# The ninth chunk's attention product as 64x64 array quarters, with even and odd heads in two PSUM banks

## The chip, the cores and the metric

The kernel runs on one core of one Trainium2 chip. The time is device microseconds of that core, as the median of several executions. Before the change it is 264.96 us, the median of 3 runs (264.48 to 265.18). One execution was also recorded by the hardware profiler; its lines are quoted below. In them PE is TensorE's matmul row, PEld its weight loads, DVE is VectorE, ACT is ScalarE, POOL is GpSimd and SP is SyncE, whose queue issues DMAs.

## What is computed

There are 8 batches, 8 heads, 576 positions and a head dimension of 64. Attention here is linear: q is normalised over the head dimension, k over the positions, and the product of k and v is a 64x64 matrix per head. After it comes a layer norm with a two-layer MLP and a residual.

```python
# q, k, v: (8, 8, 576, 64) float32; moe_w_ch1: (512, 2048); moe_w_ch2: (2048, 512)
q_s = softmax(q, axis=-1)
k_s = softmax(k, axis=2)
kv = np.einsum('bhsd,bhse->bhde', k_s, v)
x = np.einsum('bhsd,bhde->bhse', q_s, kv)            # the ninth chunk's part of this is what changes
x = x.transpose(0, 2, 1, 3).reshape(8, 576, 512)
xn = (x - mu) / np.sqrt(var + 1e-06) * g_ln
out = x + np.maximum(xn @ w_ch1, 0.0) @ w_ch2
```

## The kernel before

**Chunks.** The 8 x 576 positions are worked in nine chunks of 512, each as 4 token tiles (t = 0 to 3) of 128 positions. Chunks 0 to 7 are the first 512 positions of each batch. The ninth chunk, `C9` (number 8), gathers the 64 positions that are left of each of the eight batches: its tile t holds batch 2t in partitions 0 to 63 and batch 2t+1 in partitions 64 to 127.

**The order.** It is written out by hand. `run(main, side)` walks through the MLP steps of one chunk (`mlp_steps`, weight 0.5 for each 128x128x256 matmul) and puts in, at the places that the side list names, the attention of the next chunk and the loads of the one after. Each engine executes its instructions in the order in which they were issued. C9's attention is the side list `attn_rest` (L870) while chunk 7's MLP is the main list. It puts `po_mm` of t = 0 and 1 at place 14 and of t = 2 and 3 at place 58, `x_fast` of the four tiles at 22, 54, 66 and 75, `square_sum` at 46, 62, 69 and 77, the DMA transposes `xn_T` at 61 and 78, and `sum_x` at 102.

**The attention product.** `po_mm(c, t, i)` (L380) multiplies the transposed exponentials `eqT` of one tile and one pair of heads i (partitions 0 to 63 hold the even head's 64 dimensions, 64 to 127 the odd head's) by `kv_sb[:, batch, i, :]`, a 128x128 matrix with the two heads' 64x64 blocks on the diagonal and zeros elsewhere. In chunks 0 to 7 that is one matmul with 128 rows, 128 columns of weights and 128 moving columns. In C9 the two halves of a tile belong to two batches, so there are two matmuls (L394): 128 rows, 64 columns of weights (one batch's 64 positions), 128 moving columns. A tile t of C9 fills one PSUM buffer `po` of [128, 512] float32, one bank. The pool `att_ps` (L69) has two such banks; `po` of t = 2 takes the bank of t = 0, and t = 3 that of t = 1.

**What follows it.** `x_fast(c, t)` (L424) is one DVE instruction that multiplies the bank by the reciprocal softmax sums `rq`, writes `x` in bf16 and its row sum into `mv[:, t, 0:1]`; the row sum comes as a second record, DVE_READ_ACCUMULATOR. `xn_out` (L416) then subtracts the mean. `square_sum` (L404, ACT) gives the variance, with that row sum as its bias. `xn_T` (L274) transposes `xn` by DMA from SP's queue, tiles 0 and 1 in one and 2 and 3 in the other. `sum_x` (L244) makes the four sums `tq` of C9's transposed `xn` on DVE.

**What stands beside it.** Both layers of the MLP use seven products in place of eight (`prod1` L698, L711; `prod` L552, L566) with sums of their operands. For the second layer, `sum_h` (L539, L550) makes the sums `hs` on DVE, `copy_u` (L589, L591) copies bank `ba` to SBUF on ACT, `add_u` (L593, L594) adds such a copy on DVE (`seed_e` begins bank `be` with it), and `y_quarter` (L572, L577) makes the output quarters from the banks. The pool `mm_ps` (L70) has six banks for these. The first layer of C9 begins right behind chunk 7's second layer: its second `bb` bank is the one in which chunk 7's `ba` was.

`kv_pairs` (L343, L357) is the other place with matmuls of 64 weight columns: the product of k and v, 128 rows, 64 columns of weights, 65 moving columns, the two halves of the array's columns in turn.

Of the kernel before, what the change touches and what calls it, by code (L numbers as in the profile page):

```python
# [12 lines left out]
FP32 = mybir.dt.float32  # L13
BF16 = mybir.dt.bfloat16
AF = mybir.ActivationFunctionType
ALU = mybir.AluOpType
# [4 lines left out]
def kernel(  # L21
# [16 lines left out]
    nc = tc.nc  # L38

    B, H, S, D = q.shape  # L40
    DM = H * D
    DH = 4 * DM
    P = 128
# [5 lines left out]
    NP = H // 2  # L49
# [3 lines left out]
    C9 = B  # L53
# [15 lines left out]
    att_ps = ctx.enter_context(tc.tile_pool(name="att_ps", bufs=2, space=PS))  # L69
# [19 lines left out]
    kv_sb = const.tile([P, B, NP, P], BF16)  # L89
# [85 lines left out]
    eks, eqs, eqTs, xs, xnTs, rstds, tqs = {}, {}, {}, {}, {}, {}, {}  # L175
# [165 lines left out]
    halves = (slice(0, 64), slice(64, P))  # L341
# [36 lines left out]
    pobox = {}  # L378

    def po_mm(c, t, i):  # L380


        if i == 0:
            pool, tag = (mm_ps, "m") if c == 0 and t >= 2 else (att_ps, "a")
            pobox["p"] = pobox[c, t] = pool.tile([P, DM], FP32, tag=tag, name="po")
        if c < B:
            nc.tensor.matmul(  # L387
                pobox["p"][:, i * P : i * P + P], eqTs[c][:, t, i, :], kv_sb[:, c, i, :],
                start=True, stop=True,
            )  # L390
        else:
            for half in range(2):
                ps = slice(64 * half, 64 * half + 64)
                nc.tensor.matmul(  # L394
                    pobox["p"][ps, i * P : i * P + P], eqTs[c][:, t, i, ps],
                    kv_sb[:, 2 * t + half, i, :], start=True, stop=True,
                )

    def stats(c, t, src):
        _, st, _, mv = xs[c]  # L400
# [15 lines left out]
    def xn_out(c, t):  # L416

        x, _, xn, mv = xs[c]
        nc.vector.tensor_scalar(
            out=xn[:, t], in0=x[:, t], scalar1=float(DM), scalar2=mv[:, t, 0:1],  # L420
            op0=ALU.mult, op1=ALU.subtract,
        )

    def x_fast(c, t):  # L424

        x, st, _, mv = xs[c]
        nc.vector.scalar_tensor_tensor(  # L427
            x[:, t].rearrange("p (h d) -> p h d", h=H),
            in0=pobox[c, t].rearrange("p (h d) -> p h d", h=H), scalar=1.0,
            in1=eqs[c][2][:, t].to_broadcast([P, H, D]), op0=ALU.mult, op1=ALU.mult,  # L430
            accum_out=mv[:, t, 0:1] if c else st[:, t, 0:1],
        )
        if c:
            xn_out(c, t)
# [394 lines left out]
    def attn_fast(c):  # L829

        s = [(4 + 4 * t, lambda t=t: reduce_q(3, t, 2)) for t in (0, 2)] if c == 3 else []
        kv, new, ps, squares, ts, rstd = (
            (24, 40, ((48, 53), (57, 59), (65, 67), (73, 75)), (66, 74, 87, 91), (61, 78), 95)
            if c == 3 else
            (3, 10, ((13, 24), (48, 53), (57, 59), (65, 67)), (60, 66, 74, 87), (55, 70), 92)
        )
        s += [(22 if c == 3 else 2, lambda: recip_q(c)), (kv, lambda: kv_pairs(c)), (new, lambda: start_x(c))]
        for t, (p0, p1) in enumerate(ps):
            s += spread([lambda t=t, i=i: po_mm(c, t, i) for i in range(NP)], p0, p1)
            s += [(p1, lambda t=t: x_fast(c, t)), (squares[t], lambda t=t: square_sum(c, t))]  # L840
        s += [(ts[0], lambda: xn_T(c, 0, 2)), (ts[1], lambda: xn_T(c, 2, 2)), (rstd, lambda: rstd_op(c))]
        s += [((84, 100 if c == C9 - 1 else 88, 92, 101)[i], lambda i=i: sum_x(c, i)) for i in range(4)]
        return s

    def second_side():

        s = [(p, lambda i=i: quarter_w2(i, 1)) for i, p in enumerate((7.8, 7.9, 33.9, 66))]
        s += [(8.0, lambda: xn_pT(1, 3, nc.vector))]
        s += [(3, lambda: exp_q(2, 0, 4)), (7, lambda: exp_q(2, 2, 4)), (7.2, lambda: eq_T(2))]
        s += [(40, lambda: square_sum(1, 2)), (63, lambda: square_sum(1, 3)), (67, lambda: rstd_op(1))]  # L850
        s += [(10, lambda: load_batch(3, (2,), eqTs[2][0:1, T - 1, NP - 1, 0:4])), (31, lambda: load_batch(3, (0,)))]
        s += [(23 + j, lambda j=j: cast_v(2, j)) for j in range(2)]
        s += [(at, lambda i=i: sum_x(1, i)) for i, at in enumerate((9.1, 9.2, 31.5, 36))]
        s += [(10.1, lambda: load_v(3))]
        s += [(101 + j, lambda j=j: cast_v(3, j)) for j in range(2)]
        s += [(15 + 3 * t, lambda t=t: reduce_q(2, t, 2)) for t in (0, 2)]
        s += [(36, lambda: recip_q(2))]
        s += [(18, lambda: exp_k(2, 0, 4)), (22, lambda: exp_k(2, 2, 4)), (26, lambda: prep_kvrem(2))]
        s += [(35, lambda: kv_pairs(2))]
        s += [(40, lambda: start_x(2))]  # L860
        for t, (p0, p1) in enumerate(((42, 45), (47, 52.6), (55, 60.5), (65, 69))):
            s += spread([lambda t=t, i=i: po_mm(2, t, i) for i in range(NP)], p0, p1)
            s += [(p1, lambda t=t: x_fast(2, t)), ((69, 78, 84, 90)[t], lambda t=t: square_sum(2, t))]
        s += [(57, lambda: xn_T(2, 0, 2)), (73, lambda: xn_T(2, 2, 2)), (96, lambda: rstd_op(2))]
        s += [(74, lambda: exp_q(3, 0, 4)), (78, lambda: exp_q(3, 2, 4)), (84, lambda: eq_T(3))]
        s += [(93, lambda: exp_k(3, 0, 4)), (104, lambda: exp_k(3, 2, 4)), (109, lambda: prep_kvrem(3))]
        s += spread([lambda i=i: sum_x(2, i) for i in range(4)], 95, 108)
        return s

    def attn_rest():  # L870

        s = [(2, lambda: recip_q(C9)), (4, lambda: start_x(C9))]
        for t, (p0, p1, p2) in enumerate(((14, 22, 46), (14, 54, 62), (58, 66, 69), (58, 75, 77))):
            s += [(p0, lambda t=t: [po_mm(C9, t, i) for i in range(NP)])]
            s += [(p1, lambda t=t: x_fast(C9, t)), (p2, lambda t=t: square_sum(C9, t))]
        s += [(61, lambda: xn_T(C9, 0, 2)), (78, lambda: xn_T(C9, 2, 2)), (88, lambda: rstd_op(C9))]
        return s + spread([lambda i=i: sum_x(C9, i) for i in range(4)], 102, 104)
# [274 lines left out]
```

## Time and profile before

| what | value |
|---|---|
| median of 3 runs | 264.96 us (264.48 to 265.18) |
| the profiled execution's own time | 264.57 us |
| its span, first to last instruction | 262.8 us |
| mean granted TensorE clock | 0.998 |
| C9's `po` matmuls (L394) | 32, in two bursts of 16, begun at 211.1 and 221.4 us |
| `x_fast` on a bank (L427) | 34 instructions 128x512, 683 ns each, and 34 READ_ACCUMULATOR, 82 ns each |
| from 210 to 225 us | PE busy 15.00 of 15.00, DVE 12.18, ACT 11.65, POOL 0.18 us |
| from 225 to 235 us | PE busy 10.00 of 10.00, DVE 8.71, ACT 2.95 us |

A busy record begins where its instruction starts and lasts until its end; matmuls overlap in the array, so the distance from one start to the next is what a matmul costs, and not its record of some 220 or 270 ns. The same holds for DVE: a 128x512 instruction has a record of 0.68 us, and the next one can start 0.61 us after it.

### The profile page before, as it was taken

What the parts mean: (1) busy time and instruction counts of PE and PEld (TensorE: products, weight loads), DVE (VectorE), ACT (ScalarE), POOL (GpSimd) and SP (SyncE); (2) the same over time, 40 slices, a digit from 0 to 9 for tenths busy, and PEclk for the clock granted to TensorE, in tenths of its full rate; (3) what the DMA queues carried; (4) which work ended last, traced back from release to release, by engine and by line L of the source; (5) the groups of instructions that cost most, each with busy time, mean ns of one, the idle gap of its engine ahead of it and who ended that gap; (6) DMA issues with size and microseconds to landing.
All of it is one profiled execution on the core that took longest, in us unless ns stands there. A gap on an engine that the chain in (4) does not pass through costs nothing.

```text
span 262.8 us, 6694 instructions
## 1 busy us (share of the span) xinstructions
PE 255.6 (97%) x2624; PEld 220.0 (84%) x2627; DVE 224.0 (85%) x492; ACT 174.3 (66%) x340; POOL 94.8 (36%) x148
## 2 busy tenths in 40 slices
PE   8999989999999999999999999999999999999993
PEld 6789745789888898999899889998899888888882
DVE  6879597999999999899889988998898869977872
ACT  4557780888977885789478947894788378447400
POOL 3962228233079104930980097009000800030000
PEclk9999999999999999999999999999999999999999
DMA  6999999979958995999299929994906320321014
GB/s 193 254 205 206 356 218 283 282 185 298 170 125 265 281 140 67 284 274 129 67 301 247 167 62 278 247 169 94 266 5 127 115 81 10 73 102 60 2 41 120
DMA packets 82536, 45.00 MB, mean 171 GB/s; under 512 B 58116, under 2 KB 79112, under 8 KB 82504
## 3 DMA queue, kind: packets, MB, share of 16 engines
q0 software_dynamic: 32464, 21.76, 44.2%
q1 hardware_dynamic: 49440, 22.29, 39.0%
q10 hardware_dynamic: 600, 0.53, 0.6%
q8 instruction: 20, 0.33, 0.5%
q14 instruction: 12, 0.10, 0.1%
HBM read 36.70 MB, written 9.44 MB: 176 GB/s over the span
## 4 chain that ended last, share of the span: by engine, by line
PE 82%; DMA 9%; POOL 3%; DVE 3%; ACT 1%; issue 0%; DVEq 0%
PE ba L566 21%; PE bx L711 20%; PE bb L711 10%; DMA qt<-in_q_dram 9%; PE be L566 5%; PE bc L566 5%; PE bb L566 5%; PE bc L711 5%; PE pc L519 3%; PE po L387 2%; PE pkv L357 2%; PE ph L483 1%; DVE x L427 1%; POOL w_raw L99 1%; DVE ot L500 1%; POOL v L965 1%
## 5 line engine op out<-in xcount | busy, mean ns | idle before, releaser
L566 PEld LDWEIGHTS <-hs 128*128 128x128 bf16 x512 | 49.8, 98 | 5.7
L711 PEld LDWEIGHTS <-w_q 128*128 128x128 bf16 x480 | 45.6, 98 | 5.1
L259 POOL TENSOR_TENSOR tq<-xnT 128x256 bf16<-128x256 bf16 x26 | 17.2, 677 | 77.0 <-DMA xnT<-xn 63.0
L566 PEld LDWEIGHTS <-hT 128*128 128x128 bf16 x384 | 37.1, 98 | 4.3
L711 PEld LDWEIGHTS <-w1g 128*128 128x128 bf16 x360 | 34.1, 98 | 4.1
L711 PE MATMUL bx<-tq,w_q 128*128 128x256 bf16 x240 | 31.7, 273 | 0.0
L566 PE MATMUL ba<-w_q,hs 128*128 128x256 bf16 x256 | 30.8, 273 | 0.0
L735 ACT COPY bc<-bx 128x512 f32<-128x512 f32 x30 | 16.7, 591 | 20.8 <-PE bx L711 20.5
L742 DVE TENSOR_TENSOR bb<-bx,s 128x512 f32<-128x512 f32 x30 | 19.5, 695 | 8.4 <-ACT s L739 5.7
L583 POOL DMA_DIRECT2D out_dram<-ot x28 | 15.4, 558 | 24.2 <-DVE ot L577 24.1
L427 DVE SCALAR_TENSOR_TENSOR x<-po,rq 128x512 bf16<-128x512 f32 x34 | 23.2, 683 | 0.9 <-PE po L387 0.7
L407 ACT ACTIVATE scrap<-x,mv 128x512 bf16<-128x512 bf16 x32 | 23.0, 720 | 1.4 <-DVE x L427 1.2
L753 ACT ACTIVATE hT<-bb 128x512 bf16<-128x512 f32 x30 | 16.3, 595 | 9.9 <-PE bb L711 9.1
L745 DVE TENSOR_TENSOR hT<-bx,s 128x512 bf16<-128x512 f32 x30 | 19.3, 684 | 3.8 <-PE bx L711 3.8
L387 PE MATMUL po<-kv_sb,eqT 128*128 128x128 bf16 x128 | 22.1, 219 | 0.0
L550 DVE TENSOR_TENSOR hs<-hT 128x1024 bf16<-128x1024 bf16 x32 | 21.6, 685 | 0.5 <-ACT hT L753 0.5
L753 ACT ACTIVATE hT<-bc 128x512 bf16<-128x512 f32 x30 | 16.4, 595 | 8.4 <-PE bc L711 8.4
L218 DVE TENSOR_REDUCE zq<-eq 128x16 f32<-128x1024 bf16 (+1 forms) x20 | 20.7, 1051 | 0.0
L591 ACT COPY s<-ba 128x512 f32<-128x512 f32 x15 | 8.7, 582 | 13.3 <-PE ba L566 8.6
L753 ACT ACTIVATE hT<-bx 128x512 bf16<-128x512 f32 x30 | 16.4, 604 | 0.7 <-PE bx L711 0.7
L566 PE MATMUL ba<-w_sb,hT 128*128 128x256 bf16 x128 | 16.7, 273 | 0.0
L739 ACT COPY s<-bb 128x512 f32<-128x512 f32 x30 | 16.5, 619 | 0.0
(152 smaller groups left out, 550.3 us busy)
## 6 DMA issues: line engine op xcount, KB each, us to landing
out_dram<-ot POOLq DMA_DIRECT2D x30, 256.0 KB, 5.0
qt<-in_q_dram SPq DMA_DIRECT2D x5, 1024.0 KB, 6.7
kt<-in_k_dram SPq DMA_DIRECT2D x5, 1024.0 KB, 12.2
qt<-in_q_dram POOLq DMA_DIRECT2D x2, 1024.0 KB, 12.4
kt<-in_k_dram POOLq DMA_DIRECT2D x2, 1024.0 KB, 14.1
vm<-in_v_dram POOLq DMA_DIRECT2D x16, 128.0 KB, 12.6
w_raw<-in_moe_w_ch_dram POOLq DMA_DIRECT2D x3, 512.0 KB, 10.4
w_sb<-in_moe_w_ch_dram POOLq DMA_DIRECT2D x3, 512.0 KB, 16.2
```

The costliest lines, as they stand in the source:

```text
L218: nc.vector.reduce_sum(eqs[c][1][:, ts], eqs[c][0][:, ts], axis=AX.X)
L259: eng.tensor_tensor(out=dst[:, t], in0=x[:, t], in1=y[:, t], op=ALU.subtract)
L387: nc.tensor.matmul(pobox["p"][:, i * P : i * P + P], eqTs[c][:, t, i, :], kv_sb[:, c, i, :], start=True, stop=True,)
L407: nc.scalar.activation(scrap, x[:, t], AF.Square, bias=mv[:, t, 0:1], scale=-float(DM), accum_out=mv[:, t, 1:2],)
L427: nc.vector.scalar_tensor_tensor(x[:, t].rearrange("p (h d) -> p h d", h=H), in0=pobox[c, t].rearrange("p (h d) -> p h d", h=H), scalar=1. ...
L550: nc.vector.tensor_tensor(out=dst, in0=x, in1=y, op=op)
L566: nc.tensor.matmul(hbox[bank][:, t], lhsT, rhs, start=first and (own or t == 0) and k == 0, stop=k == KH - 1, skip_group_check=True)
L711: nc.tensor.matmul(dst[:, q], lhsT, rhs, start=first and q == 0 and ko == 0, stop=ko == 1, skip_group_check=True)
L735: nc.scalar.copy(at[g, "c"], at[g, "x"])
L742: nc.vector.tensor_tensor(out=at[g, "b"], in0=at[g, "x"], in1=at[g, "s"], op=ALU.add)
L745: nc.vector.tensor_tensor(out=h_out(g, 1, 1), in0=at[g, "x"], in1=at[g, "s"], op=ALU.add)
L753: nc.scalar.activation(h_out(g, odd, half), at[g, name], AF.Relu)
```

## The change

For C9 alone, `po_mm` does one head of one batch at a time: 64 rows (one head's dimensions, `hs`), 64 columns of weights (one batch's positions, `tok`), 64 moving columns (that head's block of `kv_sb`). The row half is given by the head's place in the pair, the column half by the batch's half of the tile, so that the four matmuls of a pair lie in four different quarters of the array. There are 64 of them for 32 before. The even heads' results go to one bank and the odd heads' to another, so a pair of tiles (t = 0 and 1, or 2 and 3) fills two banks together, both of `att_ps`: t = 2 and 3 need both banks that t = 0 and 1 filled.

`x_fast` for C9 then reads two banks: two instructions of 128x256 (as 4 heads of 64, with `x` and `rq` strided), each with a row sum of its own in `st`, and one 128x1 addition of the two. For the other chunks nothing is different.

```diff
     def po_mm(c, t, i):
+        if c == C9:
+            if i == 0 and t % 2 == 0:
+                pobox["q"] = [
+                    att_ps.tile([P, 2, NP, D], FP32, tag="a", name="po") for _ in range(2)
+                ]
+            pobox[c, t] = pobox["q"]
+            for m, tok in enumerate(halves):
+                for half, hs in enumerate(halves):
+                    nc.tensor.matmul(
+                        pobox["q"][half][tok, t % 2, i, :], eqTs[c][hs, t, i, tok],
+                        kv_sb[hs, 2 * t + m, i, hs], start=(t % 2 == 0 and i == 0), stop=True,
+                        skip_group_check=True,
+                    )
+            return
         if i == 0:
             pool, tag = (mm_ps, "m") if c == 0 and t >= 2 else (att_ps, "a")
             pobox["p"] = pobox[c, t] = pool.tile([P, DM], FP32, tag=tag, name="po")
-        if c < B:
-            nc.tensor.matmul(
-                pobox["p"][:, i * P : i * P + P], eqTs[c][:, t, i, :], kv_sb[:, c, i, :],
-                start=True, stop=True,
-            )
-        else:
-            for half in range(2):
-                ps = slice(64 * half, 64 * half + 64)
-                nc.tensor.matmul(
-                    pobox["p"][ps, i * P : i * P + P], eqTs[c][:, t, i, ps],
-                    kv_sb[:, 2 * t + half, i, :], start=True, stop=True,
-                )
+        nc.tensor.matmul(
+            pobox["p"][:, i * P : i * P + P], eqTs[c][:, t, i, :], kv_sb[:, c, i, :],
+            start=True, stop=True,
+        )
...
     def x_fast(c, t):
         x, st, _, mv = xs[c]
+        if c == C9:
+            for half in range(2):
+                nc.vector.scalar_tensor_tensor(
+                    x[:, t].rearrange("p (i two d) -> p i two d", two=2, d=D)[:, :, half],
+                    in0=pobox[c, t][half][:, t % 2], scalar=1.0,
+                    in1=eqs[c][2][:, t].rearrange("p (i two) -> p i two", two=2)[:, :, half]
+                    .to_broadcast([P, NP, D]),
+                    op0=ALU.mult, op1=ALU.mult, accum_out=st[:, t, half : half + 1],
+                )
+            nc.vector.tensor_add(mv[:, t, 0:1], st[:, t, 0:1], st[:, t, 1:2])
+            xn_out(c, t)
+            return
         nc.vector.scalar_tensor_tensor(
```

## The prediction

> **What bounds the kernel now.** I read the page's busy shares and slices first, then the chain of waits in order of time, then the timeline around the two bursts of C9's `po` matmuls.
>
> ```profile
> PE 255.6 (97%) x2624; PEld 220.0 (84%) x2627; DVE 224.0 (85%) x492; ACT 174.3 (66%) x340; POOL 94.8 (36%) x148
> PE   8999989999999999999999999999999999999993
> DVE  6879597999999999899889988998898869977872
> PEclk9999999999999999999999999999999999999999
> ```
>
> PE is full from the second slice to the last but one, at full granted clock. That row alone proves little, because matmul records overlap. The chain (start, length, what) shows that PE's own work sets the time:
>
> ```profile
> 211.22 0.57 PE po L394 x16
> ...
> 221.50 0.57 PE po L394 x16
> ...
> 226.97 1.75 PE bc L566 x16
> 228.72 1.75 PE ba L566 x16
> ```
>
> From 208 to 258 us it names nothing but PE, and a common matmul's slot is 1.75/16 = 0.109 us. So in this stage time saved or lost on PE reaches the end; DVE and ACT count only where PE comes to wait for them.
>
> **Part 1, the bursts on PE.** The timeline at the first burst, and the first and last lines of the last `kv_pairs`:
>
> ```profile
> 210.62 0.60 PE L711 MATMUL bc<-xnT,w1g 128*128 128x256 bf16 x4
> 211.15 0.64 PE L394 MATMUL po<-kv_sb,eqT 128*64 128x128 bf16 x16
> 211.72 0.61 PE L711 MATMUL bc<-xnT,w1g 128*128 128x256 bf16 x4
> ```
>
> ```profile
> 182.53 0.32 PE L357 MATMUL pkv<-vm,ek 128*64 128x65 bf16 x8
> ...
> 183.16 0.20 PE L357 MATMUL pkv<-vr,ekr 128*64 128x65 bf16 x2
> ```
>
> The last `bc` matmul ahead of the burst starts at 210.62 + 0.60 - 0.27 = 210.95, and its slot ends at 211.06. PE is back at common matmuls at 211.72. The burst therefore costs 0.66 us. Its 16 matmuls start over 0.64 - 0.22 = 0.42 us, 28 ns apart on average, about 0.45 us for all. The other 0.21 us is the way into this array shape and out of it, which I keep: the shape changes just as often.
>
> After the change a burst is 32 matmuls of 64 moving columns, in eight groups of four quarters. No row shows quarters. The nearest is `pkv`: 38 starts in 183.16 - 182.53 = 0.63 us, so 33 ns for a pair that fills both column halves with 65 moving columns, 16.6 ns each. If all four quarters run side by side, as the two column halves do, a group costs what such a pair does: 8 x 0.033 = 0.26, and with 0.21 a burst is 0.48 us, **0.18 us less**. Bounds: 0.21 us, if the matmuls cost nothing beyond the change of shape (0.45 less); 32 x 0.033 + 0.21 = 1.27 us, if each takes a pair's slot alone (0.61 more). Between them, 16.6 ns each as in `pkv`, if only two run at a time: 0.53 + 0.21 = 0.74, 0.08 more. I take 0.48, as operands, banks and quarters of four neighbours are all different.
>
> The Trainium skill (TensorE: Matmul & The Clock Gate, "Wait — 56ns, not 53.3ns?") speaks against this: starts are said never to come closer than about 25 ns, however few columns move. By that rule a burst would be 32 x 25 ns + 0.21 = 1.01 us and the two together 0.7 us longer. The `pkv` row, at 16.6 ns, is already below that floor, so it does not hold between parts of the array here; what it would give is weighed below as a mechanism of its own.
>
> **Part 2, `x_fast` on DVE.** The timelines of DVE at the second tile, and early on, where L312 has the same operation with 128x128:
>
> ```profile
> 220.71 0.68 DVE L427 SCALAR_TENSOR_TENSOR x<-po,rq 128x512 bf16<-128x512 f32 x1
> 221.32 0.08 DVE L427 DVE_READ_ACCUMULATOR x<-po,rq 128x1 f32 x1
> 221.44 0.35 DVE L419 TENSOR_SCALAR xn<-x,mv 128x512 bf16<-128x512 bf16 x1
> ```
>
> ```profile
> 11.59 0.35 DVE L312 SCALAR_TENSOR_TENSOR kv_sb<-pkv,rzk,diag 128x128 bf16<-128x128 f32 x1
> 11.86 0.09 DVE L312 DVE_READ_ACCUMULATOR kv_sb<-pkv,rzk,diag 128x1 f32 x1
> 11.98 0.25 DVE L316 TENSOR_SCALAR mbc<-ones_w,kvs 128x128 bf16<-128x128 bf16 x1
> ```
>
> From the start of `x_fast` to that of `xn_out`, 0.73 us. A 128x512 takes 0.61 until its accumulator is read, a 128x128 0.27; 128x256 by the straight line is 0.39 (L577's 128x256 follow each other by 0.40). The read costs the next instruction nothing where that does not need it (at 17.79 us it and L891 start together) and 0.12 where it does; between the halves I take 0.06. The 128x1 addition needs both sums (0.12) and holds `xn_out` by about 0.15 (L445, 128x1, is 0.143). Sum: 0.39 + 0.06 + 0.39 + 0.12 + 0.15 = 1.11, **0.38 us more** for each tile; bounds 0.30 and 0.50.
>
> **Part 3, the new wait.** Before, t = 2 took a bank that had been free since 215.2 us, and only t = 3, eight matmuls into the second burst, needed the bank of t = 1, read until 221.40. Now the second matmul of the burst needs both banks. The work between the bursts follows PE: DVE and ACT idle there waiting for `bx` and `bb` (1.1 and 0.6 us), which also swallows the 0.38 of tile 0. So `x_fast` of tile 1 starts 0.18 earlier, at 220.53. It frees the odd heads' bank after 0.39 + 0.06 + 0.39 + 0.08 = 0.92, at 221.45, and PE goes on some 0.04 later (L419 starts 0.04 after the read's end). PE would be there at 221.43 - 0.18 = 221.25. **Wait 0.24 us** (0.16 to 0.36). Queued behind it on PE are the rest of the burst and chunk 7's `ba` products.
>
> **Part 4, DVE's debt.** Tiles 1 to 3 put DVE back by 3 x 0.38 - 0.18 = 0.96 us at 226, since it has no idle time from 217.3 to 228.3. Who waits:
>
> ```profile
> 226.03 0.72 ACT L407 ACTIVATE scrap<-x,mv 128x512 bf16<-128x512 bf16 x1 [1.21 <-DVE x L427]
> 226.65 0.19 ACT L407 ACTIVATION_READ_ACCUMULATOR scrap<-x,mv 128x1 f32 x1
> 227.01 0.59 ACT L591 COPY s<-ba 128x512 f32<-128x512 f32 x1 [0.17 <-PE ba L566]
> ```
>
> The square moves to 226.99, the copy behind it to 227.81, and `ba` is free at 228.40; PE wants it at 228.72 - 0.12 = 228.60. Cover 0.20, gone if a tile costs 0.45 more rather than 0.38. The seed of `be` (L594, ends 228.33) moves to 229.29, for PE at 230.35: cover 1.06. The sums `hs` begun at 221.71 are 0.2 late with 1.1 to spare. The transpose of tiles 2 and 3 leaves SP's queue 0.96 later, at 227.3; transposes land after 3.0 at the least, as this one did, so at 230.3. `sum_x` behind it starts at 230.3 for 229.55, four of them take 0.8, and DVE is 0.05 late at 231.12, where it had idled for ACT. The read of `ba` by L577 (ended 234.97) then clears C9's second `bb` bank by about 0.1 us. A landing 0.3 later costs PE 0.2. I cost Part 4 at nothing; without these covers, up to 0.6.
>
> **Sum:** -0.18 - 0.18 + 0.24 = **-0.12 us**. On the profiled execution, span 262.8, time 264.57, that is 264.45; its time is 0.39 below the median, so on the median it is 264.8.
>
> **Rivals.**
> - *The wait does not bite*, because the first half and its read overlap further than the rows show: -0.36, 264.6. For it: DVE starts instructions before the last one's record ends. Against: the bank's second half cannot be freed before the second instruction ends. The cheapest burst of the bounds gives -0.66, again with the wait away: 264.3.
> - *The debt surfaces on PE*, at the copy of `ba` or at the late transpose: +0.1 to +0.5, 265.1 to 265.5. For it: covers of 0.20 and 0.1. Against: several must be gone by tenths.
> - *Two at a time only*: 2 x 0.08 + 0.24 = +0.40, 265.4. For it: no row shows row halves side by side.
> - *One at a time, which ends slower.* A matmul in a quarter holds the array's issue until its 64 columns have moved: 28 ns, the average of a start in `po`, to 33. Its place is both bursts, 2 x (32 x 0.028 + 0.21 - 0.66) + 0.24 = +1.13, up to +1.46: 266.1 to 266.4. It decides against the change from 10 ns a matmul on (2 x 32 x 0.010 + 0.42 + 0.24 = 1.3, what the bursts cost now) and passes +0.8 from 23 ns. Against it: 16.6 ns in `pkv`, with two halves. The skill's floor would be this rival at 265.9.
>
> **How the numbers follow.** About 0.3%, 0.8 us, is what a measurement of this kernel can tell from no change. Forecast (-0.35 to +0.1) 0.47; the wait does not bite 0.12; debt 0.10; two at a time 0.10; one at a time 0.14; another loss over 0.8 that no row shows 0.03; a gain over 0.8 0.04, since both bursts together cost only 1.32 us. So faster 0.04, same 0.79, slower 0.17. Predicted 264.8. The range leaves out most of the one-at-a-time case and the last two: from 264.1 (the cheapest burst, and 0.2 of run-to-run spread) to 266.0.
>
> **What would show it.** A burst that costs 0.48 us from slot to slot, starts of four quarters together, groups 33 ns apart. In the second burst one or two matmuls at once, then a gap of about 0.2 us whose releaser is DVE's `x`. `x_fast` to `xn_out` 1.1 us for four tiles. The square of tile 3 on ACT at about 227.0 and no gap in `ba` at 228.6 nor in `bb` at 235. The prediction is wrong if a quarter's starts are over 20 ns apart throughout, or if PE stands still in 223 to 236 us.

## The result, and the profile after

The changed kernel takes 266.31 us (median of 8 runs, 264.07 to 268.04), the kernel before 264.92 us beside it (8 runs, 264.29 to 265.18). The ratio is 1.0045, 95% interval 1.0024 to 1.0066: about 1.2 us slower, where a gain of 0.12 us was forecast. The ratios of this document leave out runs that are over 1.5% longer than the fastest of their kernel, here the one of 268.04 us and later those of 268.81 and 269.06 us of h2_after_late64. The spread is as telling as the median: without that run still 3.3 us from the shortest to the longest, where the kernel before has 0.9.

The profiled execution of the changed kernel took 265.5 us, its span is 263.7 us and its mean granted clock 0.997. First its page: busy time by engine, slices of the span, and the row of a DMA queue, `q8 instruction`, that I take for the one that fetches PE's program (packets, MB, share of 16 DMA engines).

```profile
PE 255.8 (97%) x2659; PEld 220.4 (84%) x2659; DVE 224.3 (85%) x504; ACT 174.5 (66%) x340; POOL 94.8 (36%) x148
...
PE   8899999999999999999999999999999999999992
...
DVE  6778597999999999799879988998898979977872
...
PEclk9999999999999999999999999999999999999998
...
q8 instruction: 21, 0.34, 0.5%
```

PE has 35 matmul records more (32 were added; a few are missing from either trace) and 0.2 us more of busy time, DVE 0.3 us: nothing here looks like 1.2 us. The last line was not read in the prediction. The same row of the page before the change:

```profile
q8 instruction: 20, 0.33, 0.5%
```

So PE's program arrives in packets of about 16 KB, and there is now one more. That the queue is PE's follows from the runs below: rows added on PE move its packets or add one (g2_before_plus64, e3_pad_end), DVE instructions added do not (e2_dve_alone). Hold on to that row.

The chain of waits after the change (start, length, what), for the stage that the prediction spoke of:

```profile
211.75 0.44 PE bc L729 x4
212.18 0.38 PE po L391 x32
212.56 0.54 PE bc L729 x4
...
222.27 0.48 PE po L391 x32
...
227.66 1.75 PE bc L584 x16
229.41 1.75 PE ba L584 x16
```

It still names PE alone. The `bc` piece of 227.66 stood at 226.97 before, so PE is 0.69 us late there. It was already late ahead of both bursts. The PE timelines at the first and at the second burst:

```profile
211.58 0.60 PE L729 MATMUL bc<-xnT,w1g 128*128 128x256 bf16 x4
212.11 0.45 PE L391 MATMUL po<-kv_sb,eqT 64*64 64x64 bf16 x32
212.49 0.61 PE L729 MATMUL bc<-xnT,w1g 128*128 128x256 bf16 x4
```

```profile
221.67 0.60 PE L584 MATMUL ba<-w_sb,hT 128*128 128x256 bf16 x4
222.20 0.55 PE L391 MATMUL po<-kv_sb,eqT 64*64 64x64 bf16 x32
222.68 1.05 PE L584 MATMUL ba<-w_sb,hT 128*128 128x256 bf16 x8
```

Read as in the prediction, the slot ahead of the first burst ends at 211.58 + 0.60 - 0.27 + 0.11 = 212.02, and common matmuls go on at 212.49: the burst costs 0.47 us for 0.66 before. The second costs 222.68 - (221.67 + 0.60 - 0.27 + 0.11) = 0.57. Together the bursts are 0.28 us cheaper, wait included. But the first begins 0.97 us later than before (212.02 against 211.06), and this arose before 54 us, in code that the change doesn't touch. The end of the span adds 0.25 us: from DVE's last instruction to the end of the span it is 4.1 us for 3.85. 262.8 + 0.97 - 0.28 + 0.25 = 263.7, the span. So this profile shows a gain where the change is and losses in two places where it is not.

DVE's timeline at the second tile, whose odd-head half frees the bank that the second burst waits for:

```profile
221.49 0.42 DVE L435 SCALAR_TENSOR_TENSOR x<-po,rq 128x256 bf16<-128x256 f32 x1
221.83 0.08 DVE L435 DVE_READ_ACCUMULATOR x<-po,rq 128x1 f32 x1
221.83 0.42 DVE L435 SCALAR_TENSOR_TENSOR x<-po,rq 128x256 bf16<-128x256 f32 x1
222.17 0.08 DVE L435 DVE_READ_ACCUMULATOR x<-po,rq 128x1 f32 x1
222.29 0.16 DVE L442 TENSOR_TENSOR mv<-st 128x1 f32<-128x1 f32 x1
222.49 0.35 DVE L425 TENSOR_SCALAR xn<-x,mv 128x512 bf16<-128x512 bf16 x1
```

The halves start 0.34 us apart, and `xn_out` follows 1.00 us after `x_fast` began, for 0.73 before.

### The profile page after: what moved, and what is told of

It reads as the page before. It is cut to its first block, busy times and chain, and to the rows that moved or that the text cites. A ratio compares the mean times of both kernels' runs of the same rounds, so it can differ in the third digit from the quotient of the medians.

```text
span 263.7 us, 6773 instructions
## 1 busy us (share of the span) xinstructions
PE 255.8 (97%) x2659; PEld 220.4 (84%) x2659; DVE 224.3 (85%) x504; ACT 174.5 (66%) x340; POOL 94.8 (36%) x148
## 4 chain that ended last, share of the span: by engine, by line
PE 79%; DMA 12%; DVE 4%; POOL 3%; issue 0%; ACT 0%; DVEq 0%; ACTq 0%
PE ba L584 21%; PE bx L729 20%; PE bb L729 10%; DMA qt<-in_q_dram 9%; PE be L584 5%; PE bc L584 5%; PE bb L584 5%; PE bc L729 5%; DMA ktr<-in_k_dram 3%; PE po L400 2%; PE pkv L357 2%; PE ph L501 1%; DVE x L445 1%; POOL w_raw L99 1%; DVE ot L518 1%; POOL v L983 1%
## 5 line engine op out<-in xcount | busy, mean ns | idle before, releaser
L445 DVE SCALAR_TENSOR_TENSOR x<-po,rq 128x512 bf16<-128x512 f32 x30 | 20.5, 684 | 0.9 <-PE po L400 0.7
```

The lines of the kernel that those rows point to most:

```text
L445: nc.vector.scalar_tensor_tensor(x[:, t].rearrange("p (h d) -> p h d", h=H), in0=pobox[c, t].rearrange("p (h d) -> p h d", h=H), scalar=1. ...
```

## The experiments

All ratios are against the kernel before, run on the same chip. One count is useful beside the medians: runs over 265.5 us. Of the kernel before, 14 of 124 runs were over it (all together, median 264.73); of the changed kernel 13 of the 20 that the result and the first experiment give (median 265.87).

### The first set: which part carries the loss

**e1_again**: the changed kernel once more, no edit, to see whether the loss at 54 us and that at the end come back.

> The changed kernel again. Its profile had saved about 0.18 us around the two bursts, and lost 0.9 us before 54 us, in code the change does not touch, where loads landed later. If that loss belongs to the changed program (layout), it comes back: median about 266.3, ratio about 1.004 to 1.005, and the profile again 0.5 to 1 us late at the first ph matmul (54.3 for 53.3). If the first 54 us merely vary from run to run in any kernel, the ratio is 0.998 to 1.001 and the spread is that of the kernel before.

Measured 265.69 us (264.24 to 267.04, 12 runs), ratio 1.0027 (1.0005 to 1.0049). Its profiled execution, 266.22 us, is only 0.13 late at the first burst and has an end of the usual length. It loses its time at a third place. The timeline of DVE, the last part in brackets being the idle time ahead:

```profile
228.79 0.87 DVE L595 SCALAR_TENSOR_TENSOR ot<-bc,rstd,x 128x256 f32<-128x256 f32 x2
231.95 0.49 DVE L259 TENSOR_TENSOR tq<-xnT 128x256 bf16<-128x256 bf16 x2 [2.29 <-issue]
...
235.74 0.86 DVE L595 SCALAR_TENSOR_TENSOR ot<-ba,rstd,x 128x256 f32<-128x256 f32 x2
```

and of PE behind it:

```profile
233.65 1.04 PE L729 MATMUL bx<-xnT,w1g 128*128 128x256 bf16 x8
235.87 0.60 PE L729 MATMUL bb<-tq,w_q 128*128 128x256 bf16 x4 [1.19 <-DVE ot L595]
236.66 0.60 PE L729 MATMUL bb<-tq,w_q 128*128 128x256 bf16 x4 [0.19 <-DVE ot L595]
```

DVE stands still for 2.29 us ahead of `sum_x`, which reads the late transpose; the reads of the banks (L595) come behind it, the last of them frees the bank in which C9's second `bb` goes, and PE waits for that. This is the path of Part 4. What is late is the transpose. The DMA view of 226 to 234 us for this execution (GB/s in slices of 0.2 us, the queues, median us from issue to landing):

```profile
GB/s 0 0 0 0 0 0 0 0 0 0 0 90 218 223 207 205 192 158 17 84 0 0 0 0 0 0 0 0 0 0 0 0 0 0 0 0 0 0 0 0
...
q8 instruction: 1, 0.02, 0.7%
issues: line engine op xcount, KB each, median us to landing
xnT<-xn SPq DMA_TRANSPOSE x1, 4.8
```

The same view of the kernel before:

```profile
GB/s 0 0 0 0 0 0 0 40 211 219 214 204 206 183 35 0 0 0 0 0 0 0 0 0 0 0 0 0 0 0 82 0 0 0 0 0 0 0 0 0
...
xnT<-xn SPq DMA_TRANSPOSE x1, 3.0
```

The lone 82 of the kernel before, in the slice that begins at 232.0, is the packet of PE's program (16 KB in 0.2 us is 82 GB/s; it is booked where it starts, at 232.09). The transpose had ended 2.7 us earlier. In e1_again the packet is the 84 at 229.8, right at the transpose's end. The trace gives each part of the transpose a landing: in the kernel before all sixteen come from 229.24 to 229.40 us, in e1_again fifteen from 230.14 to 230.28 and one at 231.87. The packet lasts from 229.85 to 230.78. The same view of 229.84 to 230.84 us, in slices of 25 ns, shows what the late part waits for:

```profile
DMA  9000000000000000000000000000000000000100
...
q8 instruction: 1, 0.02, 5.8%
q1 hardware_dynamic: 2, 0.00, 0.3%
```

The program's packet begins at 229.852, as the last 256-byte packet of the transpose ends (229.856). The two packets of the transpose (q1) that are left have 4 bytes each; they begin at 230.769 and 230.778, just as the program's packet ends (230.783), and the late landing follows. Theory from here on: the 64 more PE rows (32 matmuls and 32 weight loads) shift the places where PE's program is fetched, DVE's debt shifts the transpose, and they meet.

**e2_dve_alone**: the kernel before, with `x_fast` of C9 in two halves and the addition, but on one bank and with the old matmuls. It carries DVE's debt without the quarters and without the extra rows.

```diff
     def x_fast(c, t):
+        if c == C9:
+            for half in range(2):
+                nc.vector.scalar_tensor_tensor(
...
+                    in0=pobox[c, t].rearrange("p (i two d) -> p i two d", two=2, d=D)[:, :, half],
...
+            nc.vector.tensor_add(mv[:, t, 0:1], st[:, t, 0:1], st[:, t, 1:2])
```

> DVE part alone: the old 128x64 matmuls into one bank for each tile, x_fast in two halves and the addition. By my sum: t = 3's bank is free 0.38 later, the wait for it at most 0.2 us, the bursts unchanged: 265.0 to 265.3. If the program's layout sets the early loads, it may be off by up to 1.5 us in the first 54 us, with only 8 more DVE instructions. If the cost of the change lies in x_fast, it is as slow as the changed kernel, 266.3.

Measured 264.57 us (264.0 to 266.06, 12 runs), ratio 0.9992 (0.9971 to 1.0013). The transpose lands from 229.98 to 230.12, the packet comes at 232.07, PE doesn't wait. The debt alone costs nothing.

**e3_pad_end**: the kernel before, with 32 matmuls of no use behind the last product (64 more PE rows at the end of the program).

```diff
+        pad = att_ps.tile([P, 64], FP32, tag="a", name="pad")
+        for _ in range(32):
+            nc.tensor.matmul(pad[0:64], junk[:, 0:64], junk[:, 0:64], start=True, stop=True)
```

> The kernel before with 32 more small matmuls at the very end of PE's program, behind the last product, beside the last stores: nothing before 258 us differs but the length of PE's program (64 rows, as many as the change adds). Layout theory: median 265.8 to 266.8 and a wider spread, loss in the first 54 us. Otherwise 264.9, same as before within 0.1%.

Measured 265.86 us (264.43 to 268.05, 12 runs), ratio 1.005 (1.0029 to 1.0071), 10 of 12 runs over 265.5. The matmuls themselves end at 259.2 us, before the last stores have landed. The DMA view of 256 to 266 us:

```profile
q8 instruction: 1, 0.02, 0.6%
issues: line engine op xcount, KB each, median us to landing
...
out_dram<-yl SPq DMA_DIRECT2D x2, 64.0 KB, 3.9
out_dram<-yl ACTq DMA_DIRECT2D x2, 64.0 KB, 4.2
```

and of the kernel before, which has no program packet there:

```profile
out_dram<-yl SPq DMA_DIRECT2D x2, 64.0 KB, 2.3
out_dram<-yl ACTq DMA_DIRECT2D x2, 64.0 KB, 2.8
```

A 21st packet (259.95 to 260.94) runs beside the last stores, and one landing in sixteen of the last four stores comes 1.4 to 1.8 us late (of the first, 262.05 with the other fifteen by 260.22). This is a second place where the extra rows cost time, with no quarter and no DVE debt in the kernel.

**e4_null**: the kernel before with its lines moved by 18 and nothing else.

> The kernel before with only its line numbers moved by 18. Both theories: 264.9, ratio 0.999 to 1.001. If it is as slow or as spread as the changed kernel (264 to 268), then building and loading a program anew already moves the time by that much, and neither the change nor its length is the cause.

Measured 264.77 us (264.0 to 266.59, 12 runs), ratio 1.0006 (0.9988 to 1.0025): moved source lines cost nothing.

### The second set: moving the packets

A helper issues n matmuls of no use in the four quarters. Put at place 73.9 of chunk 0's MLP (about 33 us, where PE has time to spare), 32 of them move every later packet by 64 rows.

```diff
+        def pad_mm(n):
+            pad = [att_ps.tile([P, 64], FP32, tag="a", name="pad") for _ in range(2)]
+            for i in range(n):
+                hs, tok = halves[i % 2], halves[i // 2 % 2]
+                nc.tensor.matmul(
+                    pad[i % 2][tok], junk[hs, 0:64], junk[hs, 0:64], start=True, stop=True
+                )
...
+                (73.9, lambda: pad_mm(32)),
```

**g4_after_plus64**: the changed kernel with `pad_mm(32)`.

> The changed kernel with those 32 small matmuls more (64 PE rows). Fetch theory: pieces at about 226, 239 and 254, ahead of the late transpose (227 to 231) and of the last stores: 264.4 to 264.9, less than the changed kernel by 1 us or more, with more instructions. Otherwise as the changed kernel or later, 265.7 to 266.5.

Measured 264.14 us (263.62 to 264.61, 12 runs), ratio 0.9975 (0.9962 to 0.9988). Adding 32 useless matmuls makes the changed kernel 1.5 us faster than e1_again (on another chip) and 0.6 us faster than the kernel before. In its profile the packets come at 224.69, 239.16 and 253.50, clear of the late transpose (landed 229.67 to 229.82) and of the last stores. It is also 0.20 us early at the first burst.

**g2_before_plus64**: the kernel before with `pad_mm(32)`.

> The kernel before with 32 small matmuls more on PE at 33.5 us, where PE waits 0.66 us for ACT: the same PE length as the changed kernel, bursts and x_fast as before. Fetch theory: the piece of 232 us comes at about 229, on this kernel's last transpose (26.3 to 229.4 us), and a 21st at about 259, beside the last stores: 265.3 to 266.2 with a spread of 2 us or more. If the cost is in the bursts or in x_fast: 264.7 to 265.0.

Measured 264.73 us (263.98 to 267.64, 12 runs), ratio 1.0004 (0.9978 to 1.0031). The median of 265.3 to 266.2 that was expected did not come. The tail did: three runs over 265.5. The profiled one, 265.67 us, has the packet of 259.66 beside the last stores and a landing at 261.99 where the other fifteen end by 260.08. In the middle, the packet starts at 228.46 and the transpose lands from 228.77 to 228.91, with no part late: the two meet without DVE's debt as well. The extra rows alone, so placed, hit now and then only. Why e3_pad_end, with a packet at the same place of the end, moves the median and this run does not, was not seen.

**g3_before_plus128**: the same with `pad_mm(64)`.

> The kernel before with 64 small matmuls more at the same place (128 PE rows). Fetch theory: pieces 7 us earlier, the late ones at about 225, 239 and 253, clear of the last transpose and of the last stores: 264.7 to 265.2 with the spread of the kernel before, though its program is longer than that of the changed kernel. If length itself costs (memory layout, more program to load), it is slower than the one with 64 rows more: 266 to 267.

Measured 265.32 us (264.33 to 266.89, 12 runs), ratio 1.0018 (0.9998 to 1.0038), a little above what was expected. Its profiled execution has its packets clear (225.77, 240.54, 254.25), no late landing, and is 0.24 us late at the first burst. Yet 4 of the 12 runs are over 265.5; what makes them longer was not seen, and it speaks against the packets as the only reason for long runs.

**g1_after_less64**: the changed kernel with 64 PE rows fewer, by leaving out the products ko 4 to 11 of chunk 0's second layer.

```diff
-                for t in range(T) for ko in range(k0, k0 + kn)
+                for t in range(T) for ko in range(k0, k0 + kn) if not 4 <= ko < 12
```

> The changed kernel with 64 PE rows fewer (32 weight loads, 32 matmuls): of chunk 0's second layer the products of ko = 4 to 11 are left out, at a place (35 to 49 us) where the loads set the pace. Fetch theory (PE's program comes in 16 KB pieces, about every 256 PE rows; the 64 added rows move the piece of 232 us onto the late transposes of tiles 2 and 3 and bring a 21st piece beside the last stores): the pieces are back where the kernel before has them, no 21st piece, so 264.4 to 264.7, ratio 0.998 to 1.000, spread under 1.5 us. If the change's own instructions (bursts, x_fast, debt) cost the time, it stays at 265.7 to 266.3.

Measured 271.8 us (270.88 to 272.37, 6 runs), ratio 1.0257 (1.0233 to 1.0282). This says nothing of the packets. The busy table by stage (us, PE busy with count, granted clock, DMA share, GB/s) of this run:

```profile
34.00:50.00 16.00, 7.87 (x51) 0.79 1.19 249
50.00:100.00 50.00, 47.89 (x530) 0.93 0.83 187
```

With PE idle for half of 34 to 50 us, the granted clock falls to 0.79 there and is 0.93 up to 100 us; in the profile of the changed kernel both stages have 1.00. Less work went with about 6 us more. A count of rows has to be changed where PE stays busy.

### The third set: one meeting at a time, and other ways to move

**h1_tile3_early**: `x_fast` of tile 3 at place 67.5 for 75 and its transpose at 70 for 78, so that the transpose is early; the length of the program is left as it is.

```diff
-        for t, (p0, p1, p2) in enumerate(((14, 22, 46), (14, 54, 62), (58, 66, 69), (58, 75, 77))):
+        for t, (p0, p1, p2) in enumerate(((14, 22, 46), (14, 54, 62), (58, 66, 69), (58, 67.5, 77))):
...
-        s += [(61, lambda: xn_T(C9, 0, 2)), (78, lambda: xn_T(C9, 2, 2)), (88, lambda: rstd_op(C9))]
+        s += [(61, lambda: xn_T(C9, 0, 2)), (70, lambda: xn_T(C9, 2, 2)), (88, lambda: rstd_op(C9))]
```

> The changed kernel with x_fast of tile 3 ahead of two of chunk 7's sums hs (place 67.5 for 75) and its transpose at place 70: the late transpose leaves SP 1.2 us earlier, at about 225.9, and lands at about 229, before the piece of PE's program at 230. The 21st piece at the end stays. If the loss of the changed kernel is at the transpose, 264.3 to 264.7; if it is at the last stores, 265.3 to 266; if each has a part, between.

Measured 264.64 us (264.15 to 267.17, 11 runs), ratio 1.0008 (0.9986 to 1.003); 2 of 11 runs over 265.5. The edit did not part the two: in its profile the transpose lands from 228.63 to 228.77, 1.2 us earlier than in i3_look below, but the packet comes 1.1 us earlier too, at 228.37. What it gives is more time for a late landing. The last packet comes at 263.58, after the end of the span.

**h2_after_late64**: the changed kernel with `pad_mm(32)` at place 14 of C9's own MLP (about 237 us), so that the packet near the transpose stays and the one at the end moves (to 254.13).

```diff
-        run(mlp_steps(C9), [(33 + 3 * i, lambda i=i: sum_h(0, i)) for i in range(2)])
+        run(mlp_steps(C9), [(33 + 3 * i, lambda i=i: sum_h(0, i)) for i in range(2)]
+            + [(14, lambda: pad_mm(32))])
```

> The changed kernel with 32 small matmuls more on PE inside C9's first layer (about 237 us), where PE sets the time: they cost 0.47 us as a burst does. The piece at 230 us stays where it is, beside the transpose; the last one moves from 258 to about 254.5, ahead of the last stores. If the end alone is the loss, 264.4 + 0.5 = 264.9 with a small spread; if the transpose is the loss, 265.9 to 266.5.

Measured 265.08 us (264.29 to 269.06, 12 runs), ratio 1.0016 (0.9991 to 1.0042); 5 of 12 runs over 265.5, four of them over 266.5. Of the 10 that the ratio counts, it is 3. The useless matmuls cost 0.47 us from slot to slot, 0.0018 of the ratio; less that, it is about 0.9998, beside 1.0008 in h1. Both expectations that named one place are missed, 265.9 to 266.5 for the transpose and a small spread for the end. With counts this small, neither run singles out a place.

**h3_both**: g4 and h1 together.

> Tile 3 early and the 64 more PE rows at 33.5 us together: transpose and last stores are both clear of the pieces, and the debt is smaller. 264.0 to 264.2, the same as with the 64 rows alone (264.14): nothing was left to gain at the transpose there.

Measured 264.2 us (263.62 to 264.77, 12 runs), ratio 0.9981 (0.9969 to 0.9994). With the packets clear, moving tile 3 adds nothing to g4.

**h4_warm18**: the changed kernel with 32 PE rows fewer and no work left out: the 34 warm-up matmuls at the start become 18 longer ones.

```diff
-    junk = const.tile([P, 256], BF16)
+    junk = const.tile([P, 512], BF16)
...
-        warm(34)
+        warm(18, 484)
```

> The changed kernel with 32 PE rows fewer, without leaving out work: the first warm-up as 18 matmuls of 484 columns for 34 of 256 (8712 columns for 8704). PE's program ends before a 21st piece, and the piece of 230 comes at about 231, behind the landing of the transpose. 264.2 to 264.6, spread under 1.5 us. If length does not matter, 265.7 to 266.3 as the changed kernel.

Measured 264.13 us (263.53 to 265.19, 12 runs), ratio 0.9983 (0.997 to 0.9995). The packet comes at 229.69, behind the landings of 229.23 to 229.37, and none is recorded at the end. It is 0.66 us early at the first burst. Of the 36 runs of g4, h3 and h4 none was over 265.5.

**i1_before_warm18**: the same warm-up in the kernel before.

> The kernel before with the warm-up as 18 matmuls of 484 columns, 32 PE rows fewer. If the gain of the changed kernel with that warm-up (264.13) comes from the quarters (0.1 to 0.2 us in the bursts, and nothing lost), this one is at 264.3 to 264.8. If the warm-up alone brings it, it is at 264.0 to 264.2.

Measured 264.57 us (264.01 to 266.19, 12 runs), ratio 1.0003 (0.9982 to 1.0024). The warm-up by itself brings no gain that this can tell. h4 is 0.44 us shorter, on another chip; the bursts explain 0.28 us of it, the rest is not shown.

**i2_look, i3_look, i4_look**: three single executions of the changed kernel, each with its profile.

> The changed kernel once more, for where a single execution loses time. Fetch theory: one over 265.3 us shows one of 16 landings of the late transpose over 1 us after the others, with a gap on PE at 234.5 to 237 behind it, or one landing of the last stores over 1 us after the others; one under 264.8 shows neither.

> As the look before: a slow execution has a late landing at the transpose or at the last stores, a fast one has neither.

> As the two looks before: a slow execution has a late landing at the transpose or at the last stores, a fast one has neither.

They took 265.1, 264.17 and 267.44 us. i4_look is e1_again over again, in its DVE and PE timelines:

```profile
232.50 0.49 DVE L259 TENSOR_TENSOR tq<-xnT 128x256 bf16<-128x256 bf16 x2 [2.32 <-issue]
```

```profile
236.42 0.60 PE L729 MATMUL bb<-tq,w_q 128*128 128x256 bf16 x4 [1.21 <-DVE ot L595]
237.21 0.60 PE L729 MATMUL bb<-tq,w_q 128*128 128x256 bf16 x4 [0.19 <-DVE ot L595]
```

The packet runs from 230.40 to 231.33, fifteen landings come from 230.71 to 230.85, the sixteenth at 232.42. PE's work behind `bb` slips by about 1.7 us: the records show 1.40 of idle time, and a record is longer than its slot. It is also 0.66 us late at the first burst, and another 0.8 us of its time lies outside the span (267.44 - 264.84 = 2.60 us, 1.78 in i2_look and i3_look). i3_look is the same program without any of this, in its DVE timeline:

```profile
230.08 0.49 DVE L259 TENSOR_TENSOR tq<-xnT 128x256 bf16<-128x256 bf16 x2 [0.57 <-issue]
```

DVE is idle for 0.57 us, PE does not wait, and its first burst begins at the same 211.05 us as in the kernel before. Its last DVE instruction ends 0.29 us earlier (258.65 for 258.94): the local gain of 0.28 arrives at the end undiminished. i2_look, 265.1 us, has no late landing at either place; it is 0.85 us late at the first burst, from before 54 us. So the one execution over 265.3 us and the one under 264.8 came out as expected; i2_look lies between the two and tests nothing.

## Why the prediction was wrong

**The bursts (Part 1): right.** 0.471 us against 0.48, and the same to 0.001 in all eleven profiles that hold the quarters. Single starts in the trace: four quarters within 10 ns, groups 32 ns apart (33 was taken), and 0.22 us for the shape change (0.21). The rivals of two and of one at a time are refuted.

**`x_fast` (Part 2): mis-sized.** 0.27 us more a tile and not 0.38, below the lower bound of 0.30. The halves follow each other after 0.34, not after 0.39 + 0.06: the straight line through 128x512 and 128x128 was too dear, and the accumulator's read does not hold up the second half. The addition was a little dearer than thought: 0.34 + 0.34 + 0.12 + 0.20 = 1.00, where 0.15 was taken for the last term.

**The wait (Part 3): right in kind, mis-sized.** It was taken as 0.24. The second burst shows one matmul, then a gap; it costs 0.576, so the wait is 0.576 - 0.471 = 0.105 us. `x_fast` of tile 1 starts where it was said to (220.53 in the time of the kernel before), but takes 222.25 - 221.49 = 0.76 until the bank is free, not 0.92. So the sum of the first three parts is -0.19 - 0.09 = -0.28 us, more than twice the -0.12 that was forecast. Had nothing else happened, the kernel would have been faster by 0.1%. g4, h3 and h4 are faster by 0.2%; their profiles are early at the first burst too, by 0.20, 0.45 and 0.66 us.

**DVE's debt (Part 4): the step that failed.** "I cost Part 4 at nothing" is right for the debt by itself: e2_dve_alone, i3_look, and the copy of `ba` on ACT (228.33 us, PE's next `ba` at 229.41) show no wait. The debt was even smaller than forecast: the transpose leaves SP 0.62 us later, not 0.96, in line with 3 x 0.27 - 0.18 = 0.63. The step rested on one number, that the transpose lands 3.0 us after its issue "at the least", and treated that as what it will be. A late landing was priced ("0.3 later costs PE 0.2") along the right path, from `sum_x` over L577 (now L595) to C9's second `bb` bank, but the size taken was 0.3 us and not 1.8 (4.8 for 3.0), with 0.10 for the whole rival and a ceiling of 0.5 us. In e1_again and i4_look it is 1.7 us on PE. The other three profiles of the changed kernel have no late landing there.

**The term that was missing.** The 64 new PE rows were counted as time in the array and never as program. That program is fetched by the same DMA engines: 20 packets over the 5251 rows that the trace records, one per 260 or so, 11 to 14 us apart late in the run, 0.9 to 1.4 us each. 64 rows more pull the packet of 232.1 us to about 229.5 to 230.5 us, while the debt pushes the late transpose to meet it there. A 21st packet can fall beside the last stores: of the five profiles of the changed kernel it does in one (258.33 to 259.47, landings up to 0.45 us late); two have it after the end of the span, two not at all. The Trainium skill (Runtime: NRT & Kernel Launch, "Instruction fetch mechanics") states blocks of 16 KiB, 256 instructions, fetched ahead through a DMA queue of the engine's own, with the cost "mostly hidden". The row of 20 packets and 0.33 MB agrees in size and number. As to the cost: PE was not seen waiting for its program, so there it is hidden; the transfer that shares the time with the packet pays.

**How far this is shown.** Shown: adding 64 rows at 33 us or leaving out 32 at the start, which moves the packets, takes the loss away with the quarters and the debt in place (0.9975, 0.9983); neither edit gains anything in the kernel before (1.0004, 1.0003). The debt alone costs nothing (0.9992). The rows alone cost nothing at 33 us, but at the end of the program as much as the whole change (e3_pad_end, 1.005). Shown too, by the packets and landings in the traces: late parts go with packets of the program. In the 18 profiles a packet of q8 starts within 1 us ahead of a transpose's first landing 49 times, and in 26 of these some landing comes over 1 us after the first. Among the 328 other transposes whose landings are all recorded there is no such case. Ten of the 26 have one late landing alone, as in e1_again; in each of the ten the last 4-byte packet of the transpose begins 2 to 5 ns ahead of the end of the program's packet. The kernel before has one of them, at 75.63 us with the last landing at 77.28, so the meeting is not new; its place is. From this order I infer that packet and late part share one of the 16 DMA engines; the trace does not name the engine.

A meeting in time is not enough: at the late transpose it took place in eight profiles, with the packet 0.25 to 0.37 us ahead of the first landing, and in two of them a part was late. In the other six the transpose's last packet had begun at most 0.06 us after the program's packet.

Open: how the loss in the median divides between the transpose, the last stores and the start of the program. Three of the five profiles of the changed kernel as it stands are 0.66 to 0.97 us late at the first burst, all of it from before 54 us, in code that the change doesn't touch; i2_look (265.1 us) is longer by that alone. All other profiles but that of g1_after_less64 lie between -0.66 and +0.24, h1 and h2 among them, whose program is the same up to there. Whether the late starts are chance or belong to the loss is not shown.

**The chances.** Slower had 0.17, nearly all of it on quarters that would run one at a time, which the `pkv` row had spoken against. The range's upper end of 266.0 came from there too, and was passed for a reason that no rival held: the debt's rival had the right path, with a ceiling of +0.5 and no thought of the program's packets. The 12 runs of e1_again have a median of 265.69, inside the range.

## What to carry to other kernels

Where a DMA has only tenths of a microsecond of cover, look which other transfers run in that window, the fetch of the program among them: the row of the instruction queue and the GB/s slices show where its packets fall. An edit that adds or removes some dozens of PE instructions moves every later packet, so a wide spread of the new kernel's runs is a hint to try the same edit with a handful of instructions more or fewer ahead of it. Here the edit was worth 0.28 us in the trace, and 32 useless matmuls ahead of it 1.5 us in the median.

## What the runs showed of the hardware

- Four 64x64 quarters work fully side by side: 32 matmuls of 64 moving columns in 8 x 32 ns, 8 ns each. In e3_pad_end, 32 matmuls of 128 rows that all use the same 64 columns start 32 ns apart, each by itself (from 258.01 to 259.01 us).
- A program packet of 16 KB takes 0.9 to 1.4 us late in the run (up to 1.9 earlier). A transpose's or a store's part that meets one can be late by 1.4 to 1.9 us (e1_again, i4_look, e3_pad_end, g2_before_plus64), and the whole transfer is complete only with that part.
- With PE idle for half of a 16 us stage, the granted clock was 0.79 there and 0.93 in the 50 us after it; with 32 matmuls left out the kernel was 2.6% longer than the kernel before (g1_after_less64).
